# Folding the cast sequence of the first two batches before stage 1 of an FNet + GEGLU kernel, with small tables on ScalarE and idle matmuls between the folds

## The chip, the core and the metric

The kernel runs on one core of one Trainium2 chip. The metric is the device time of one execution in microseconds (us), and lower is better.

The engines are named as in the profile: PE is TensorE (matmuls), PEld its weight loads, DVE is VectorE, ACT is ScalarE, POOL is GpSimd, SP is SyncE.

## The reference

```python
def _attn_ref(x):                       # x: [8, 3008, 256] float32
   X = np.fft.fft(x, axis=1)            # along the sequence
   X = np.fft.fft(X, axis=2)            # along the channels
   return X.real.astype(np.float32)

def _moe_ref(x, w_gate, w_val, w_out):  # x: [24064, 256], d_ff = 1536
   g = x @ w_gate
   gelu = 0.5 * g * (1.0 + erf(g * inv_sqrt2))
   val = x @ w_val
   return (gelu * val @ w_out).astype(np.float32)
```

The second function gets the result of the first as 24,064 tokens of 256 channels.

## The kernel before

For each of the 8 batches the kernel makes the Fourier transform by matmuls, in steps:

1. *Stage 1* is the first part of the sequence transform. It contracts over 94 rows of x (3008 = 94 × 32), with a table `G` of sines and cosines. It ends in a buffer `A_sb`.
2. The *channel stage* (`ch`) combines the halves of the channels with small identity matrices `II`, while it swaps rows and columns. It ends in `Z_sb`.
3. `tp_e`, `tp_o` and `tp_y` finish the transform with a table `TP`. They end in `EO_sb` and `EB_sb`.
4. The feed-forward part runs in 36 slots per batch: gate matmuls (`ps_g`), value matmuls (`ps_v`), and in between the second layer (`ps_o`) of the chunk before. The channel transform is multiplied into the weights by `make_w`, from a table `CW`.

The opening does batch 0's transform alone, because nothing else can run yet. From then on a list of "fill" and "pool" work per slot puts the transform of the next batch between the matmuls of the feed-forward part. The time at which the first gate matmul starts is therefore a good measure of the opening.

Batches 2 to 7 are *folded* on POOL before stage 1: the sequence transform of real data has a symmetry that lets the kernel add and subtract each row x and its mirrored row, and each channel and its mirrored channel, and then contract half as much. Batches 0 and 1 are not folded. Their x is cast to bf16 on the way in (`xb`, forward rows and mirrored rows), and stage 1 does the sum inside PE, with two matmuls per row group, the second one with mirrored rows and with a `G` whose one half is negated:

```python
    G = const_pool.tile([NP, NJ, 2, 4 * NK], BF16)      # [..., 0, :] and a negated copy in [..., 1, :]

    def s1(b, jg, half, hl, engine="A"):
        def run():
            ...
            for q, js in enumerate(JG[jg][2 * half : 2 * half + 2]):
                for j in js:
                    for i in range(2):                  # i = 0: forward rows, 1: mirrored rows
                        src = _sub(xb[b], [[1, 128]], (i * NJ + (16 - j if i else j)) * C + hl * 128, part_num=NP)
                        nc.tensor.matmul(
                            _sub(ps, [[192, 2], [1, 96]], q * 96), src, _sub(G, [[96 * i, 2], [1, 96]], j * 192),
                            start=(j == js[0] and i == 0), stop=(j == js[-1] and i == 1))
            ...                                         # evict 128x384 to A_sb on ACT or DVE
```

The opening of the kernel before, cut:

```python
        pool_consts(); index_consts(0); cast_mirror(0, 9, 8)       # POOL: constants and DMA issues
        index_consts(1); cast_mirror(0, 0, 1); cast_forward(0, 1, 8)
        pool_consts2()                                             # the row "par" for the TP table
        cast_mirror(0, 5, 4); cast_mirror(0, 1, 4)
        ...                                                        # weights
        for _ in range(12):                                        # idle matmuls
            nc.tensor.matmul(ps[:, :], idle[:, 0:128], idle[:, :], start=True, stop=True)
        vec_consts(); g_phases(); vec_fills()                      # DVE
        g_sin(9, 7); g_sin_ends(); g_sin(1, 8)                     # ACT
        stage_cast(9, 4, 0); stage_cast(13, 4, 4); stage_cast(0, 1, 8); g_negative(9, 8)    # DVE
        t_columns(); t_phases(); ...; cw_phases(); ...
        stage1(2, 0); stage1(2, 1); identities(); stage1(3, 0); stage1(3, 1)
        cw_rest(); t_write()
        stage1(1, 0); stage1(1, 1); stage1(0, 1); stage1(0, 0)
        ch(0, 0)(); ch(0, 1, "V")(); make_w(0, 0, 256, engine="V")(); ...
```

"Idle matmuls" multiply a zeroed tile and are thrown away. They serve only to keep PE busy.

## Time and profile before

| | before |
|---|---|
| time, median of the 3 runs given | 646.64 us (646.18 to 647.09) |
| span of the profiled execution | 644.7 us |
| PE busy | 628.5 us, 97% of the span |
| first gate matmul starts | 28.17 us |
| granted clock 0.50 | from 9.9 to 27.0 us, and before 6.5 us |
| stage 1 of batch 0 | 68 matmuls, 9.70 to about 21.5 us |

Part 4 of the page of the kernel before is the chain of waits: the work that ended last, followed back. Its first line gives shares of the span by engine.

```profile
PE 86%; ACT 4%; POOL 3%; DVE 2%; DMA 2%; issue 1%; SPq 0%; ACTq 0%; POOLq 0%; DVEq 0%
```

PE sets the time. The next view has the windows of the kernel before: each line is a stretch of 10 us, with the busy time and the number of instructions of PE, PEld, DVE, ACT and POOL, then the granted PE clock, the DMA share and GB/s.

```profile
10.00:20.00 10.00, 9.21 (x59) 8.36 (x57) 7.98 (x31) 5.03 (x11) 8.96 (x12) 0.50 0.97 131
20.00:30.00 10.00, 8.89 (x65) 6.73 (x64) 4.64 (x7) 4.09 (x10) 0.00 (x0) 0.65 1.14 185
...
60.00:70.00 10.00, 9.70 (x78) 7.13 (x78) 6.51 (x11) 7.93 (x18) 4.40 (x4) 1.00 0.20 39
70.00:80.00 10.00, 10.00 (x82) 6.83 (x80) 8.81 (x14) 7.16 (x15) 7.50 (x8) 1.00 0.98 243
```

From 70 us on, PE is busy. So whatever a change of the first two batches gains, it gains before 70 us. Between 10 and 20 us PE seems 92% busy, but at half its clock: a busy PE is not a fast PE. The timeline of PE in the opening of the kernel before shows it; its columns are start and duration in us, engine, line, operation, out<-in, shape, number of instructions, and, in brackets, the idle time ahead and what ended it.

```profile
1.19 5.30 PE L753 MATMUL ps_o<-gelu_sb 128*128 128x512 bf16 x12 [1.19 <-DVE col L295]
8.50 1.27 PE L364 MATMUL ps_v<-one,par 1*128 1x1 f32 x10 [2.00 <-POOL par L272]
9.70 0.64 PE L463 MATMUL ps_g<-G,xb 94*128 94x192 bf16 x4
...
20.68 0.84 PE L463 MATMUL ps_g<-G,xb 94*128 94x192 bf16 x4
...
22.18 0.93 PE L488 MATMUL ps_v<-II,A_sb 128*128 128x129 bf16 x7 [0.42 <-DVE A_sb L471]
...
28.17 0.61 PE L621 MATMUL ps_g<-EO_sb,W_sb 128*128 128x512 bf16 x2
```

Groups of four stage-1 matmuls start 0.64 us apart, 160 ns for each. Batch 1's stage 1 has the same matmuls, in between the feed-forward work and at the full clock. Two lines of it, from the same view later on:

```profile
49.42 0.49 PE L463 MATMUL ps_dft<-G,xb 94*128 94x192 bf16 x4 [0.58 <-ACT A_sb L469]
50.83 0.83 PE L463 MATMUL ps_dft<-G,xb 94*128 94x192 bf16 x8
```

Four more matmuls take 0.34 us longer, about 85 ns for each by these rounded lines; the starts in the trace are 82 ns apart, and 68 of them are 5.6 us of PE. The first line also shows PE waiting for an eviction of stage 1. All waits of PE between 42 and 75 us in the kernel before (columns: who waits, for what, total us, times, longest):

```profile
PE ps_dft L463 <- ACT A_sb L469: 1.2, 2, 0.6
PE ps_dft L568 <- ACT W_sb L420: 0.7, 1, 0.7
PE ps_dft L463 <- ACT EO_sb L553: 0.5, 1, 0.5
PE ps_dft L463 <- ACT EB_sb L571: 0.3, 1, 0.3
```

### The profile page before, as it was taken

The numbers are of one execution on the slowest core, as the hardware profiler recorded it, in microseconds if no ns is written. First come the engines' busy times: TensorE is split into PE (matmuls) and PEld (weight loads), VectorE is DVE, ScalarE is ACT, GpSimd is POOL, SyncE is SP. The second block draws the span as 40 slices with busy tenths as digits, with TensorE's granted clock in tenths as the row PEclk, the third lists the DMA queues.
The fourth block names the chain that finished last, engine by engine and source line by source line (L and its number), as shares of the span: only waits on it lengthen the run. The fifth ranks groups of instructions, "written<-read, shape, count | busy, mean of one in ns | idle before, by whom it ended". The sixth has DMA issues, their size and how long they took to land.

```text
span 644.7 us, 13198 instructions
## 1 busy us (share of the span) xinstructions
PE 628.5 (97%) x4381; PEld 420.7 (65%) x4381; DVE 586.0 (91%) x944; ACT 434.4 (67%) x852; POOL 496.8 (77%) x498
## 2 busy tenths in 40 slices
PE   7988999999999999999999999999999999999997
PEld 4645767666666666666666666666666666666666
DVE  8587888999989999999999999999999999999992
ACT  4587777676676667776776667766677666666661
POOL 8174699979988799978998799987998655556651
PEclk8699999999999999999999999999999999999999
DMA  8950736444526425533445436463222332221223
GB/s 154 150 81 2 190 104 154 116 110 111 140 62 171 120 49 149 135 103 107 109 97 146 99 99 148 94 152 95 56 53 45 93 93 58 58 46 35 49 50 79
DMA packets 51994, 63.85 MB, mean 99 GB/s; under 512 B 7783, under 2 KB 47194, under 8 KB 49530
## 3 DMA queue, kind: packets, MB, share of 16 engines
q1 hardware_dynamic: 45238, 47.23, 30.3%
q0 software_dynamic: 6096, 15.29, 11.5%
q8 instruction: 34, 0.56, 0.4%
q10 hardware_dynamic: 592, 0.49, 0.3%
q14 instruction: 34, 0.28, 0.1%
HBM read 38.86 MB, written 29.38 MB: 106 GB/s over the span
## 4 chain that ended last, share of the span: by engine, by line
PE 86%; ACT 4%; POOL 3%; DVE 2%; DMA 2%; issue 1%; SPq 0%; ACTq 0%; POOLq 0%; DVEq 0%
PE ps_o L694 35%; PE ps_g L621 27%; PE ps_v L621 17%; PE ps_dft L507 2%; DMA out_dram<-out_sb 2%; PE ps_dft L543 1%; ACT gelu_sb L637 1%; POOL eo_sb L214 1%; POOL h_sb L670 1%; PE ps_dft L463 1%; ACT gelu_sb L646 1%; PE ps_dft L488 1%; DVE v_sb L668 1%; PE ps_dft L410 1%; PE ps_dft L573 0%
## 5 line engine op out<-in xcount | busy, mean ns | idle before, releaser
L670 POOL TENSOR_TENSOR h_sb<-gelu_sb,v_sb 128x512 bf16<-128x512 bf16 (+1 forms) x288 | 329.7, 1147 | 129.1 <-DVE v_sb L668 96.4
L694 PE MATMUL ps_o<-Wo_sb,h_sb 128*128 128x256 bf16 (+1 forms) x2232 | 334.7, 273 | 0.0
L694 PEld LDWEIGHTS <-h_sb 128*128 128x128 bf16 (+1 forms) x2304 | 228.8, 100 | 111.0 <-POOL h_sb L670 1.5
L655 DVE SCALAR_TENSOR_TENSOR ve_sb<-EB_sb,yw,ps_v 128x512 f32<-128x512 bf16 (+1 forms) x288 | 212.4, 737 | 37.8 <-PE ps_v L621 36.2
L637 ACT ACTIVATE gelu_sb<-ps_g 128x512 bf16<-128x512 f32 (+1 forms) x288 | 169.6, 589 | 92.7 <-PE ps_g L621 92.0
L621 PE MATMUL ps_g<-EO_sb,W_sb 128*128 128x512 bf16 (+1 forms) x864 | 230.7, 376 | 0.8 <-ACT gelu_sb L646 0.5
L621 PE MATMUL ps_v<-EO_sb,W_sb 128*128 128x512 bf16 (+1 forms) x576 | 214.5, 375 | 0.0
L666 DVE TENSOR_TENSOR h_sb<-gelu_sb,ps_v 128x512 bf16<-128x512 bf16 (+1 forms) x288 | 195.4, 678 | 0.6 <-PE ps_o L694 0.3
L668 DVE SCALAR_TENSOR_TENSOR v_sb<-ve_sb,ps_v 128x512 f32<-128x512 f32 (+1 forms) x288 | 192.9, 670 | 0.0
L621 PEld LDWEIGHTS <-W_sb 128*128 128x128 bf16 x1440 | 137.0, 98 | 77.9 <-issue 1.6
L646 ACT ACTIVATE gelu_sb<-ps_g 128x512 bf16<-128x512 f32 (+1 forms) x288 | 168.4, 585 | 0.0
L713 ACT ACTIVATE out_sb<-ps_o 128x512 f32<-128x512 f32 x92 | 55.0, 597 | 34.5 <-PE ps_o L694 33.9
L214 POOL TENSOR_TENSOR eo_sb<-ab_sb 94x512 bf16<-94x512 f32 (+1 forms) x60 | 66.6, 1111 | 0.1
L510 ACT ACTIVATE S_sb<-ps_dft 96x512 bf16<-96x512 f32 x48 | 28.2, 588 | 21.0 <-PE ps_dft L507 21.0
L553 ACT ACTIVATE EO_sb<-ps_dft 128x512 bf16<-128x512 f32 (+1 forms) x44 | 26.0, 591 | 23.2 <-PE ps_dft L543 21.2
L207 POOL TENSOR_TENSOR ab_sb<-x_raw,x_raw 94x508 f32<-94x508 f32 (+1 forms) x30 | 33.0, 1101 | 0.0
L210 POOL TENSOR_TENSOR ab_sb<-x_raw,x_raw 94x508 f32<-94x508 f32 (+1 forms) x30 | 33.0, 1099 | 0.0
L507 PE MATMUL ps_dft<-eo_sb,G 94*96 94x256 bf16 x102 | 19.2, 274 | 1.8 <-POOL eo_sb L214 1.2
L158 POOL DMA_INDIRECT x_raw<-in_x_dram,idx x18 | 17.1, 949 | 2.9 <-issue 1.1
L463 PEld LDWEIGHTS <-xb 94*128 94x128 bf16 x136 | 15.4, 121 | 4.7 <-issue 3.6
L543 PE MATMUL ps_dft<-TP,Z_sb 128*128 128x128 bf16 (+1 forms) x184 | 17.6, 218 | 0.4 <-ACT W_sb L416 0.4
L543 PEld LDWEIGHTS <-Z_sb 128*128 128x128 bf16 x192 | 15.1, 100 | 2.1 <-issue 0.3
(127 smaller groups left out, 188.9 us busy)
## 6 DMA issues: line engine op xcount, KB each, us to landing
out_dram<-out_sb SPq DMA_DIRECT2D x361, 64.0 KB
x_raw<-in_x_dram SPq DMA_DIRECT2D x10, 768.0 KB
Z_sb<-z SPq DMA_DIRECT2D x6, 768.0 KB
z<-S_sb SPq DMA_DIRECT2D x6, 576.0 KB
EB_sb<-yrow SPq DMA_DIRECT2D x14, 128.0 KB
x_raw<-in_x_dram SPq DMA_DIRECT2D x2, 640.0 KB
z<-S_sb SPq DMA_DIRECT2D x6, 192.0 KB
EB_sb<-yrow SPq DMA_DIRECT2D x7, 120.2 KB
```

Source lines behind the costliest of these rows:

```text
L207: eng.tensor_tensor(ab(0, 1, up), fwd(1, up), mir(255, down), op=ALU.add)
L214: eng.tensor_tensor(_sub(eo, [[C, nj], [1, 128]], j0 * C + g * 128), ab(0, 0, [[1, 128]]), ab(1, 0, [[1, 128]]), op=op)
L543: nc.tensor.matmul(ps[:, o : o + n], st["Z"][:, pair, g * 128 : g * 128 + 128], _sub(TP, [[1, n]], g * 128), start=True, stop=True)
L621: nc.tensor.matmul(ps[:, :n], W[nm, part][:, fs], src, start=start, stop=stop, **kw)
L637: nc.scalar.activation(gl[:, 0, :n], pg[:, :n], AF.Gelu)
L646: nc.scalar.activation(_sub(gl, [[-1, n]], TOK + n - 1), pg[:, :n], AF.Gelu)
L655: nc.vector.scalar_tensor_tensor(ve[:, :n], EB_bufs[b][:, c0 : c0 + n], yw[:, fc : fc + 1], pv[:, :n], op0=ALU.mult, op1=ALU.add)
L666: nc.vector.tensor_tensor(st["h"][:, fc, 0, :n], gl[:, 0, :n], pv[:, :n], op=ALU.mult)
L668: nc.vector.scalar_tensor_tensor(_sub(vv, [[-1, n]], n - 1), ve[:, :n], 2.0, pv[:, :n], op0=ALU.mult, op1=ALU.subtract)
L670: nc.gpsimd.tensor_tensor(st["h"][:, fc, 1, :n], gl[:, 1, :n], vv[:, :n], op=ALU.mult)
L694: nc.tensor.matmul(pso[:m, half], st["h"][:, fc, sign, h0 : h0 + m], Wo_sb[:, fc, :], start=(fc == 0), stop=(fc == NFC - 1),)
L713: nc.scalar.activation(_sub(osb, [[1, 2 * C]], 0, part_num=m), pso[:m, :], AF.Copy)
```

## The change

The intent is to fold batches 0 and 1 too, so that their stage 1 has half as many matmuls with half as many columns. DVE folds batch 0 in the opening, POOL folds batch 1 in slots 6 to 18. To make room on DVE, the small tables (identities, parts of `CW`, `TP`) move to ACT, and 24 more idle matmuls keep PE busy while DVE folds (36 in all). `par` is made earlier on POOL. The channel stage of these two batches takes the folded halves with half as many matmuls of twice the columns, and batch 2's loads and first folds move by two or three slots. The core of the diff:

```diff
-    G = const_pool.tile([NP, NJ, 2, 4 * NK], BF16)
+    G = const_pool.tile([NP, NJ, 4 * NK], BF16)
@@ fold_ops: batches 0 and 1 write a and b straight to eo
+        half = b < 2
+            if half:
+                return _sub(eo, [[C, nj]] + pat, j0 * C + q * 128 + c0)
+        if half:
+            return [first, second]
         return [first, second, combine(0, ALU.add), combine(1, ALU.subtract)]
@@ s1
-                    for i in range(2):
-                        src = _sub(xb[b], [[1, 128]], (i * NJ + (16 - j if i else j)) * C + hl * 128, part_num=NP)
-                        nc.tensor.matmul(
-                            _sub(ps, [[192, 2], [1, 96]], q * 96), src, _sub(G, [[96 * i, 2], [1, 96]], j * 192),
-                            start=(j == js[0] and i == 0), stop=(j == js[-1] and i == 1))
+                    nc.tensor.matmul(
+                        ps[:, q * 96 : (q + 1) * 96], eo[:, j, g, :], G[:, j, :],
+                        start=(j == js[0]), stop=(j == js[-1]))
@@ identities: on ACT
-            nc.vector.tensor_scalar(II[:, i, 0:128], row, col_p, sign, op0=ALU.is_equal, op1=ALU.mult)
+        nc.scalar.activation(eye, row_c, AF.Abs, scale=-1.0, bias=col_p)
+        nc.scalar.activation(II[:, 0, 0, :], eye, AF.Relu, scale=-1.0, bias=1.0)
... (CW and TP likewise)
@@ opening
         cast_mirror(0, 9, 8)
+        pool_consts2()
         index_consts(1)
         cast_mirror(0, 0, 1)
         cast_forward(0, 1, 8)
-        pool_consts2()
...
-        for _ in range(12):
-            nc.tensor.matmul(ps[:, :], idle[:, 0:128], idle[:, :], start=True, stop=True)
+        warm(9)
+        vec_fills()
         vec_consts()
         g_phases()
...
+        t_sin()
+        warm(15)
         cw_phases()
         cw_sin()
...
+        t_write()
         identities()
         cw_rest()
+        fold_piece(9, 4)
+        stage1(2)
+        warm(4)
+        fold_piece(13, 4)
+        fold_piece(0, 1)
+        stage1(3)
+        warm(5)
+        fold_piece(5, 4)
+        stage1(1)
+        warm(3)
+        fold_piece(3, 2)
+        fold_piece(1, 2)
+        stage1(0)
@@ plan
+        slot_of = [6 + i * 13 // len(ops) for i in range(len(ops))]     # batch 1's folds on POOL
-        for k, s in ((0, 16), (1, 16), (2, 17)):
+        for k, s in ((0, 18), (1, 19), (2, 19)):
             at(fill, s, lambda k=k: load_part(2, k))
-            first, n = (s0 - 16, 29) if b == 2 else (s0 - 22, 32)
+            first, n = (s0 - 13, 29) if b == 2 else (s0 - 22, 32)
```

## The prediction

> **What bounds the kernel now.** From about 70 us on, TensorE (PE) has no gaps (windows view: 10.00 busy in every 10 us; the chain of waits is 86% PE), and the change leaves that part's matmuls alone. What can move is the first 70 us (timeline):
> - x arrives by DMA (mean DMA share about 1.0 from 5 to 30 us). Stage 1 of batch 0 is 68 matmuls, 94x192, from 9.7 to 21.5 us, 160 ns start to start: half speed. The granted clock is 0.50 from 9.9 to 27.0 us.
> - 22.2 to 28.2 us: channel stage, W tables, transposes; the first gate matmul (ps_g) starts at 28.17 us.
> - Batch 1's stage 1, between 48 and 69 us at full clock: 68 matmuls at about 82 ns = 5.6 us of PE, and PE waits about 2 us for evictions (A_sb, EO_sb, EB_sb) around them.
>
> **What the change does.**
> - Stage 1 of batches 0 and 1: 34 matmuls of 96 columns each. The 128-column matmuls of the channel stage, a weight load each, run at about 56 ns, so I estimate 34 x 56 = 1.9 us, against 5.6.
> - Batch 1: 8 evictions of 128x384 instead of 16 on ACT, and about 12 us of folds on POOL (1.26 us per 94x508 operation, as L207), in slots where POOL is 45 to 65% busy.
> - Batch 0: DVE loses the casts of stage (2.8 us), negatives (0.74), identities and CW (1.7), TP (0.54), seven evictions (3.9); it gains the folds. The 94x408 fp32 operation took 0.57 us, so I estimate 0.65 per 508 elements, 1.3 per four-row piece, 6 us in all.
> - par comes earlier on POOL, so the remaining DMA issues come about 2 us earlier.
> - 24 more idle matmuls on PE. The Trainium skill (TensorE: Matmul & The Clock Gate, Part 1) says activity over a window of about 3.4 us lifts the clock from half to full, and idleness drops it. The trace agrees in the levels (12 idle matmuls at 427 ns each, later 512-column ones at 217) and the window (0.50 lasts 17.07 us, five times 3.41), but 94-row matmuls streaming from 14 to 21 us did not lift it. I expect mostly full clock from about 10 us.
>
> **The critical path after.** DVE reaches the folds at about 9 us and ends them at 15 to 15.5, near the arrival of the last mirrored rows (13 to 14). Last A_sb eviction: 16.3. Channel stage to first gate takes about 4.5 us at full clock instead of 6.0: first gate at 20.5 to 22 us, 6 to 7.5 earlier. W rows from 512 land about 22 to 23 us (bytes over GB/s), just in time. Batch 1 gains 3.5 to 5 us more. The dense rest keeps its length; I allow 1 us for new POOL waits.
>
> **Predicted: 636.0 us (-1.6%), range 631.0 to 641.0. Faster by over 2%: 0.28; within 2%: 0.71; slower: 0.01.**
>
> **What would show each step.** First ps_g at 20.5 to 22 us; granted clock 1.0 between 10 and 27 us; DVE folds at 9 to 15.5 us, about 0.6 us per large operation; stage 1 of batch 1 near 2 us of PE; DVE, not PE, before the last stage-1 matmuls; gapless PE from 70 us.
>
> **What would make it wrong.** The clock stays at 0.50 (then the idle matmuls delay stage 1: +2 to 3 us); weights land late and the gain turns into waits for w_raw; POOL folds lag, holding h_sb or batch 1's stage 1; DVE folds slower beside POOL; batch 2's later loads and folds stall PE near 100 us.

## The result and the profile after

| | before | after |
|---|---|---|
| time, median (range), 4 runs each | 646.41 us (646.10 to 647.09) | 635.34 us (634.99 to 635.73) |
| ratio | | 0.9828 (95% interval 0.981 to 0.9845) |
| span of the profiled execution | 644.7 us | 633.9 us |
| first gate matmul | 28.17 us | 22.70 us |

The change makes the kernel 1.7% faster. That is less than the 2% at which a verdict of "faster" begins, so its class is "same"; but the whole interval lies below 1, so the gain is clear of the noise. The outputs are right.

The two timelines can be laid side by side at the start of each gate matmul group, which both kernels have in the same order (289 starts). The table gives the start in the kernel before, and how much earlier the kernel after is at the same group. It is worked out from the two timelines.

| gate group | before | after | earlier by |
|---|---|---|---|
| 0 | 28.17 | 22.70 | 5.47 |
| 8 | 46.81 | 41.28 | 5.53 |
| 12 | 57.30 | 48.69 | 8.61 |
| 20 | 78.02 | 66.74 | 11.28 |
| 28 | 95.56 | 85.60 | 9.96 |
| 72 | 189.80 | 178.83 | 10.97 |
| 288 (end) | 628.88 | 618.01 | 10.87 |

The gain has two parts of almost the same size: 5.5 us in the opening, and about 5.4 us while batch 1's transform runs. After that the difference wavers between 9.7 and 11.5 us and ends at 10.87.

**The opening.** The timeline of PE in the kernel after, to compare with the one of before:

```profile
1.19 4.02 PE L757 MATMUL ps_o<-gelu_sb 128*128 128x512 bf16 x9 [1.19 <-DVE one L290]
5.27 2.29 PE L371 MATMUL ps_v<-one,par 1*128 1x1 f32 x10
7.49 6.02 PE L757 MATMUL ps_o<-gelu_sb 128*128 128x512 bf16 x15
13.34 0.34 PE L467 MATMUL ps_g<-G,eo_sb 94*128 94x96 bf16 x4
...
16.40 0.81 PE L757 MATMUL ps_o<-gelu_sb 128*128 128x512 bf16 x3
17.05 0.34 PE L467 MATMUL ps_g<-G,eo_sb 94*128 94x96 bf16 x4
17.22 0.33 PE L467 MATMUL ps_v<-G,eo_sb 94*128 94x96 bf16 x4
18.19 0.61 PE L489 MATMUL ps_dft<-II,A_sb 128*128 128x256 bf16 x4 [0.64 <-ACT A_sb L473]
...
22.70 0.61 PE L622 MATMUL ps_g<-EO_sb,W_sb 128*128 128x512 bf16 x2
```

Stage 1 now starts 3.6 us later (13.34 against 9.70), but ends 4 us earlier. From the channel stage to the first gate it takes 4.51 us instead of 6.0, because the clock is full. A note on reading the clock: the page shows a clock of 1.00 from the start of this execution, but that is only because the record begins with its first change. The idle matmuls of line 1 ran 427 ns apart, which is half speed. The first recorded change is at about 12.8 us, and the 15 idle matmuls of line 3 agree: at 427 ns each they would take 6.4 us, at 213 ns 3.2 us, and they took 5.85 us until stage 1.

Ahead of stage 1 stand DVE's folds. DVE's timeline in the kernel after, cut:

```profile
3.67 1.36 DVE L322 TENSOR_SCALAR ff<-ff 94x24 f32<-94x24 f32 x1
...
7.59 0.16 DVE L372 COPY parc<-ps_v 128x5 f32<-128x5 f32 x1 [0.90 <-PE ps_v L371]
...
11.02 0.68 DVE L217 TENSOR_TENSOR eo_sb<-x_stage,xb 94x508 bf16<-94x508 f32 x1
11.62 0.68 DVE L220 TENSOR_TENSOR eo_sb<-xb,x_stage 94x508 bf16<-94x508 bf16 x1
...
14.50 0.41 DVE L217 TENSOR_TENSOR eo_sb<-xb 94x508 bf16<-94x508 bf16 x1
14.84 0.41 DVE L220 TENSOR_TENSOR eo_sb<-xb 94x508 bf16<-94x508 bf16 x1
...
16.06 0.28 DVE L220 TENSOR_TENSOR eo_sb<-xb 94x254 bf16<-94x254 bf16 x1
```

The folds begin at 10.93 us and end at 16.34. A large fold operation costs 0.60 us start to start where one input is fp32, and 0.34 us where both are bf16. Two delays ahead of them stand out. The wait for `parc` is one: PE's ten small matmuls that make it ran at half clock and took 2.29 us, against 1.27 before. The first line is the other: 94x24 elements took 1.36 us. The same operation in the kernel before, and the instruction of POOL that runs beside it after:

```profile
2.60 0.17 DVE L311 TENSOR_SCALAR ff<-ff 94x24 f32<-94x24 f32 x1
```

```profile
3.44 1.56 POOL L281 IOTA par<- 1x128 f32 x1
```

POOL's instruction runs from 3.44 to 5.00 us, and DVE's ends at 5.03. The Trainium skill ("SBUF — State Buffer", section "Who interferes with whom") says that DVE and GpSimd share a pair of ports, that `tensor_scalar` can take it in its two-port modes, and that "whoever issues first gets the shared pair for the whole instruction". The trace agrees: 1.36 us beside that IOTA, 0.17 us without it. Moving `par` forward on POOL put it beside this operation. The kernel before has such a clash elsewhere: beside its own `par` IOTA, DVE's cast of 96x1024 elements took 1.83 us, and the next one of the same size 0.79 us.

The two delays don't add up. `parc` could not be ready before PE's `par` matmuls ended, at 7.56 us. The slow 94x24 operation lies ahead of the wait for it: without the 1.19 us that it lost, DVE would have waited 2.1 us instead of 0.9, and the folds would have begun at the same time.

At the other end, ACT's timeline of the kernel after shows the first and the last eviction of stage 1 there:

```profile
15.38 0.47 ACT L473 ACTIVATE A_sb<-ps_g 128x384 bf16<-128x384 f32 x1
...
17.61 0.53 ACT L473 ACTIVATE A_sb<-ps_g 128x384 bf16<-128x384 f32 x1
```

The first result of stage 1 was there at about 13.7 us, but ACT made tables until 15.38 and then evicted seven times without a pause. The last two evictions, on ACT and on DVE, ended at 18.15. So it is ACT's queue that sets the start of the channel stage, and not the folds. The chain of waits of the kernel after, from the view that follows it back from the last instruction (start, us, engine, tile, line, number), goes through ACT, and no fold is on it:

```profile
5.27 2.30 PE ps_v L371 x10
...
10.32 0.44 DVE small L261
10.78 0.42 ACT CW L349
...
15.48 2.66 ACT A_sb L473 x7
18.19 0.61 PE ps_dft L489 x4
```

ACT starts its tables when DVE's `small` table is there, DVE makes that after `parc`, and `parc` comes from the `par` matmuls. PE ran without a gap from 7.49 to 17.55 us, so it never waited for a fold: each group of stage 1 came 0.7 to 1.6 us after its fold was ready, behind idle matmuls. Three of these (0.65 us) stand between the last fold (16.34) and the last stage-1 group (17.05). The run e1 below takes the later idle matmuls away, and ACT's evictions and the channel stage stay where they are.

**Batch 1.** One line of PE's timeline in the kernel after, and PE's waits there between 42 and 75 us:

```profile
53.80 0.34 PE L467 MATMUL ps_dft<-G,eo_sb 94*128 94x96 bf16 x4
```

```profile
PE ps_g L622 <- ACT gelu_sb L647: 1.2, 3, 0.6
PE ps_dft L467 <- ACT EB_sb L572: 0.7, 1, 0.7
```

Stage-1 matmuls are now 43.5 ns apart (groups of five take 0.38 us, of four 0.34), so 34 of them are 1.5 us instead of 5.6. That is 4.1 us. PE's waits in these 33 us fall from 2.7 to 1.9 us. Together that is 4.9 of the 5.4 us; I don't place the last half microsecond.

**What comes back.** Two windows of the kernel after:

```profile
70.00:80.00 10.00, 10.00 (x74) 6.66 (x73) 8.51 (x13) 7.73 (x16) 6.43 (x8) 1.00 1.01 261
80.00:90.00 10.00, 9.67 (x74) 6.63 (x73) 8.50 (x14) 6.74 (x15) 10.00 (x10) 1.00 0.29 81
```

PE has no gap from 60 us on but one of 0.33 us near 83 us (and one of 1.2 us near 124 us, which the kernel before has as well, near 128). That gap comes from POOL, whose waits between 70 and 130 us have this line:

```profile
POOL ab_sb L216 <- DMA x_raw<-in_x_dram,idx: 2.0, 1, 2.0
```

In the kernel before the same wait is 0.5 us. POOL is ready for batch 2's fold before the gather of its mirrored rows has landed, and then runs late with `h_sb`.

### The profile page after: what moved, and what is told of

Same layout as the page of the kernel before. It is cut to its first block, busy times and chain, and to the rows that moved or that the text cites. A ratio compares the mean times of both kernels' runs of the same rounds, so it can differ in the third digit from the quotient of the medians. Undisturbed runs are those within 1.5% of the kernel's fastest.

```text
span 633.9 us, 13022 instructions
## 1 busy us (share of the span) xinstructions
PE 620.3 (98%) x4289; PEld 409.6 (65%) x4289; DVE 582.4 (92%) x937; ACT 433.0 (68%) x855; POOL 505.8 (80%) x511
## 3 DMA queue, kind: packets, MB, share of 16 engines
q0 software_dynamic: 6096, 15.29, 11.5%
## 4 chain that ended last, share of the span: by engine, by line
PE 85%; POOL 5%; ACT 5%; DVE 3%; issue 1%; POOLq 0%; ACTq 0%; DVEq 0%
PE ps_o L695 35%; PE ps_g L622 27%; PE ps_v L622 17%; POOL h_sb L671 3%; PE ps_dft L508 2%; PE ps_dft L544 2%; DVE v_sb L669 1%; ACT gelu_sb L638 1%; POOL eo_sb L224 1%; ACT gelu_sb L647 1%; PE ps_dft L489 1%; PE ps_dft L574 0%; DVE ve_sb L656 0%; ACT W_sb L423 0%; ACT A_sb L473 0%
## 5 line engine op out<-in xcount | busy, mean ns | idle before, releaser
L757 PE MATMUL ps_o<-gelu_sb 128*128 128x512 bf16 x36 | 13.1, 529 | 1.2 <-DVE one L290 1.2
```

## The experiments

Theories are told in words here; the quoted expectations give some of them letters. "First gate" is the start of the first gate matmul in the profiled execution, and "end" is the start of the last gate group against the kernel before. All kernels but one gave right results.

### e1_no_idle: the changed kernel without the later idle matmuls

The theory (A in the quotes) is that the idle matmuls earn their place by lifting the clock for the channel stage. The rival is that they only stand in front of stage 1.

```diff
-        warm(15)
         cw_phases()
         ...
         stage1(2)
-        warm(4)
         fold_piece(13, 4)
         fold_piece(0, 1)
         stage1(3)
-        warm(5)
         fold_piece(5, 4)
         stage1(1)
-        warm(3)
```

> The changed kernel without its 27 later idle matmuls (only the first nine stay). Theory A (the idle matmuls carry the clock): the granted clock stays 0.50 until about 25 us, the part from channel stage to first gate takes about 6 us again instead of 4.5, first ps_g at 24 to 25 us instead of 22.7, time 1 to 2.5 us longer than the changed kernel, about 637. Rival B (they only hold the queue: stage 1 began at 13.34 us although its first fold was ready at 12.3): first ps_g up to 1 us earlier, time about 634.5.

Measured: 637.91 us (636.86 to 638.12), ratio 0.985 (0.9833 to 0.9867), so about 0.2% worse than the changed kernel's 0.9828 (1.4 us by the ratios, 2.6 us by the medians of different rounds). The two intervals overlap, so the traces have to carry the reading. Two lines of PE's timeline in e1_no_idle:

```profile
11.77 0.50 PE L467 MATMUL ps_g<-G,eo_sb 94*128 94x96 bf16 x4 [4.20 <-DVE eo_sb L217]
...
18.20 1.03 PE L489 MATMUL ps_dft<-II,A_sb 128*128 128x256 bf16 x4 [1.30 <-ACT A_sb L473]
```

Stage 1 began 1.6 us earlier, at 11.77, as the rival says. But the channel stage began at the same time (18.20 against 18.19), and the way from there to the first gate took 6.0 us instead of 4.5, at half clock: first gate 24.19 against 22.70. So the idle matmuls delay stage 1, that delay costs nothing, and the clock that they bring is worth 1.5 us at the first gate. The delay costs nothing because ACT is later still: its seven evictions began at 15.40 us in e1 and the last at 17.62, against 15.38 and 17.61, and PE stood 1.30 us for them. At the end e1 is 8.49 us ahead of the kernel before, 2.4 us less than the change; part of the rest is PE's wait behind batch 2's gather, 1.2 us instead of 0.33. One of the four executions (636.86 us, mean clock 0.988 against 0.998 or 0.999) had another course of the clock; see e8_early_rows below.

### e2_before_idle: the kernel before with 15 more idle matmuls

This asks what the clock alone is worth, without any fold.

```diff
         gelu_table()
+        ps = psum("o")
+        for _ in range(15):
+            nc.tensor.matmul(ps[:, :], idle[:, 0:128], idle[:, :], start=True, stop=True)
         stage1(2, 0)
```

> The kernel before with 15 idle matmuls ahead of its unfolded stage 1 and nothing else. Theory A (half of the gain of the opening is the clock, not the folding): clock 1.0 from about 13 us, stage 1 at 82 ns a matmul, 5.6 us instead of 10.9, first ps_g near 24 us instead of 28.2, time about 642.5. Rival B (the opening's gain comes from halving stage 1): stage 1 only starts later, first ps_g at 28 us or later, time 646 to 649.

Measured: 645.11 us, ratio 0.9969 (0.9951 to 0.9988). One line of PE's timeline in e2_before_idle:

```profile
14.63 0.49 PE L463 MATMUL ps_g<-G,xb 94*128 94x192 bf16 x4
```

The clock was full from about 13.4 us. Stage 1 ran at 83 ns per matmul instead of 160, but began at 14.63 instead of 9.70, and ended at about 20.8 us. First gate 25.90, 2.27 us earlier; end 1.56 us earlier. I had expected more from the clock alone. A faster stage 1 is worth 5.2 us (68 × 77 ns), and 4.9 of it are paid for by its later start, behind the queue of idle matmuls. What remains is mostly the way from the channel stage to the first gate, 4.2 us (from 21.70) instead of 6.0. In the changed kernel the channel stage has to wait for ACT anyway (e1), so the idle matmuls cost nothing there.

### e3_fold1_only and e4_fold0_only: each batch's fold alone

e3 has the old opening and batch 0 unfolded, and batch 1 folded on POOL; e4 has the new opening, and batch 1 as before (its tables are made on POOL when that is idle).

```diff
 e3:
-        half = b < 2
+        half = b == 1
 e4:
-        half = b < 2
+        half = b < 1
 (both: old stage 1 and channel stage kept beside the new ones, as s1_old and ch_old; old G, old identities as I3)
```

> Batch 1 alone folded (on POOL), the opening of batch 0 as before. If the two parts add up: first ps_g at 28.2 us as before, and the 5.3 us that the changed kernel gains after its first gate stay, time about 641.2. Rival: those 5.3 us come in part from the earlier opening (data and weights there sooner), then under 3 us of gain, time 643.5 or more.

> Batch 0 alone folded with the idle matmuls, batch 1 unfolded as before (its tables made on POOL while that is idle). If the parts add up: first ps_g at 22.7 us, gain about 5.5 us kept to the end, time about 641. Rival: the opening's gain is swallowed by later waits when batch 1's stage 1 is unfolded, gain under 3.5 us, time 643 or more.

| | time | ratio | first gate earlier by | end earlier by |
|---|---|---|---|---|
| e3 (batch 1) | 641.28 us | 0.9912 (0.9893 to 0.9931) | -0.25 us | 5.21 us |
| e4 (batch 0) | 640.54 us | 0.9892 (0.9875 to 0.9908) | 5.19 us | 5.26 us |
| both (the change) | 635.34 us | 0.9828 (0.981 to 0.9845) | 5.47 us | 10.87 us |

The parts add up: 5.21 and 5.26 are 10.47 us, against 10.87. The ratios agree within their noise: gains of 0.88% and 1.08% are 1.96%, against 1.72%, with intervals of about 0.2% each. In e4 the difference stays between 5.19 and 5.41 us at every gate group, so nothing of the opening's gain is lost later. In e3 it is -0.25 us until group 8 and then grows to 5.53 by group 20. The 5.4 us of the result are batch 1's fold, as read.

### e5_idle94 and e6_idle192: what an idle matmul needs to lift the clock

In the kernel before, 68 dense matmuls of stage 1 (94 rows) did not lift the clock from 9.9 to 21.5 us. The rows theory (R in the quotes) says that matmuls over 94 of the 128 rows don't count enough. The columns theory (C) says that it is their 192 columns, too short for PE to be busy throughout. e5 keeps the 512 columns and takes 94 rows; e6 keeps the 128 rows and takes 192 columns, in 8/3 as many matmuls.

```diff
 e5:
-                nc.tensor.matmul(ps[:, :], idle[:, 0:128], idle[:, :], start=True, stop=True)
+                nc.tensor.matmul(ps[:, :], idle[:NP, 0:128], idle[:NP, :], start=True, stop=True)
 e6:
-            for _ in range(n):
-                nc.tensor.matmul(ps[:, :], idle[:, 0:128], idle[:, :], start=True, stop=True)
+            for _ in range(n * 8 // 3):
+                nc.tensor.matmul(ps[:, 0:192], idle[:, 0:128], idle[:, 0:192], start=True, stop=True)
```

> The changed kernel, its idle matmuls over 94 rows instead of 128 (same count, same 512 columns). Theory R (a matmul over 94 rows, like stage 1 of batches 0 and 1, does not lift the clock): clock stays 0.50 until after 20 us, the 15 idle matmuls run at 427 ns to 13.9 us, stage 1 and the channel stage at half speed, first ps_g at 24.5 us or later, time as without them or worse, 637.5 to 639. Rival C (it is the short 192-column matmuls with their gaps that do not): as the changed kernel, clock full from about 12 to 13 us, time within 0.5 us of it.

> The changed kernel, its idle matmuls over 128 rows but 192 columns each (8/3 as many, so the same columns). Theory R: clock full from about 12 to 13 us as in the changed kernel, time within 0.5 us of it. Rival C: clock stays 0.50 until after 20 us, time 637.5 to 639.

e5: 640.94 us, ratio 0.9906 (0.9889 to 0.9922); first gate 28.09. e6: 636.11 us, ratio 0.9836 (0.9819 to 0.9853); first gate 21.73. Two lines of PE's timeline in e5_idle94:

```profile
7.49 6.58 PE L757 MATMUL ps_o<-gelu_sb 94*128 94x512 bf16 x15
13.86 0.53 PE L467 MATMUL ps_g<-G,eo_sb 94*128 94x96 bf16 x4
```

In e5 PE had no gap from 7.5 to 21.9 us, and yet the clock rose only at about 27 us, after the 128-row matmuls of the channel stage, which began at 22.2. In e6 it rose at about 4 us. So 94 rows against 128 make the difference, and 192 columns against 512 don't: theory R holds, C falls. With idle matmuls that don't lift the clock the opening's gain is gone (0.08 us left): they stand in front of stage 1 at half speed, so that it ended at about 21.9 us instead of 17.55, and the rest of the opening stays slow as well.

e6's first gate came 1 us earlier than in the changed kernel, but its time is no better. It was 12.26 us ahead of the kernel before at group 20, and 9.28 at group 28. The gather of batch 2 landed after 12.8 us (11.5 in the changed kernel), POOL stood 3.7 us for it and PE 2.0 us for POOL. What is won in the opening is partly given back there.

### v1_opening: another order of the opening

An attempt to beat the change: the first fold and its stage 1 before the `TP` and `CW` tables, the identities first on ACT, `par` made after the forward rows' DMA is issued, row 0 last, 12 idle matmuls at first.

```diff
+        fold_piece(9, 4)
         t_columns()
         ...
-        warm(15)
+        warm(3)
+        stage1(2)
         cw_phases()
         ...
+        warm(14)
         fold_piece(13, 4)
-        fold_piece(0, 1)
-        stage1(3)
         fold_piece(5, 4)
         stage1(1)
         ...
+        fold_piece(0, 1)
+        stage1(3)
```

> The changed kernel with its opening reordered: the forward rows and the mirrored ones are asked for before the column constants where nothing needs those first, the first fold comes before the table phases on DVE, the identities at the head of ScalarE, 12 idle matmuls first (so that the clock can rise near 6.5 us), column groups in the order of arrival. Theory (DVE and the arrival of the mirrored rows at 14.4 us set the end of the folds): folds end at 14.5 instead of 16.3 us, first ps_g at 20 to 21 us instead of 22.7, time 633 to 634. Rival (the weights' arrival sets the pace once the first gate comes before 22 us): first ps_g earlier, but the third gate pair no earlier than 25.5 us, time 635.

Measured: 636.25 us, ratio 0.9835 (0.9819 to 0.9852), first gate 22.59: no gain. One line of DVE's timeline in v1_opening says why:

```profile
8.13 0.19 DVE L216 TENSOR_TENSOR eo_sb<-x_stage,xb 94x8 bf16<-94x8 f32 x1 [2.64 <-DMA xb<-in_x_dram,idx]
```

DVE was ready early and stood for 2.64 us, until the first mirrored rows had landed at 8.1 us; the tables that could have filled this time came after, and the last piece was folded at 17.2. My miss was to move a fold ahead of data that were not there.

### v2_later_fold2: a failed schedule

This is v1_opening with the first fold of batch 2 one slot later, against the wait for its gather.

```diff
-            first, n = (s0 - 13, 29) if b == 2 else (s0 - 22, 32)
+            first, n = (s0 - 12, 29) if b == 2 else (s0 - 22, 32)
```

> The reordered opening, and batch 2's first fold one slot later, so that POOL does not stand 2.0 us at 76 us waiting for rows of x, with h_sb products behind it. If that wait costs what PE shows (0.33 us before ps_o at 83 us): 0.3 us better than the reordered opening alone. Rival: PE is fed anyway, or the later folds lengthen the 1.2 us stall on eo_sb at 124 us: 0 to 1 us worse.

The result was wrong (relative error 0.147), so its time (644.38 us, ratio 0.9955) tells nothing. Worked out from the slots, and not tested by a run: batch 2's last use of `eo` in stage 1 slips to slot s0+17, in which batch 3's fold writes `eo` and is emitted first. The program is then free of races, but in the wrong order. Only the comparison of the result found it.

### e7_tables_dve: the small tables back on DVE

The theory (D) says that the move of the tables to ScalarE is worth about 2 us, because DVE is on the path to the folds. The Trainium skill ("ScalarE: Activation LUTs", section "Rules for kernel authors") advises the other way for such simple operations: for `relu`, `add` and `mul`, VectorE and not ScalarE. The trace agrees that VectorE is faster: DVE made these tables in 1.8 us in e7 (9.94 to 11.71), ACT in 2.8 us in the changed kernel (12.61 to 15.38).

```diff
-        nc.scalar.activation(eye, row_c, AF.Abs, scale=-1.0, bias=col_p)
-        nc.scalar.activation(II[:, 0, 0, :], eye, AF.Relu, scale=-1.0, bias=1.0)
+        nc.vector.tensor_scalar(II[:, 0, 0, :], row_c, col_p, None, op0=ALU.is_equal)
 (CW and TP likewise)
```

> The changed kernel with its small tables (identities, CW columns, TP) written by DVE as before, ahead of the folds, not by ScalarE. Theory D (the folds on DVE set the time of stage 1, so DVE is the engine to relieve): about 2 us of table work goes in front of the folds, they end at 17.5 to 18.3 us instead of 16.3, first ps_g 1 to 1.8 us later, time 636.2 to 637.2. Rival S (ScalarE, busy with tables until 15.4 us and then with eight evictions until 18.1, sets it): first ps_g no later, time within 0.4 us of the changed kernel or better.

Measured: 637.31 us (635.69 to 638.09), ratio 0.9847 (0.9832 to 0.9861). The interval overlaps that of the change (0.981 to 0.9845): a cost of 1 to 2 us, not a sure one. In the profiled execution the folds began at 11.71 us and ended at 16.55 (theory D had expected 17.5 to 18.3), and the first gate came at 23.47, 0.77 us later than in the changed kernel. Two lines of PE's timeline in e7_tables_dve show that this difference is not the tables' alone:

```profile
6.62 3.41 PE L756 MATMUL ps_o<-gelu_sb 128*128 128x512 bf16 x15
12.54 0.50 PE L466 MATMUL ps_g<-G,eo_sb 94*128 94x96 bf16 x4 [2.50 <-DVE eo_sb L217]
```

Here the clock rose at about 5.6 us, not at 12.8. The 15 idle matmuls were over at 10.0, PE stood for 2.5 us, and the clock fell back from 12.4 to 15.9 us. This is the next point.

### e8_early_rows: batch 2's forward rows loaded early

This is the changed kernel, with the loads of batch 2's forward rows moved from slots 18 and 19 to slots 10 and 12. The theory (G) says that the gather of mirrored rows lands late because the forward rows share the DMA with it.

```diff
+        for k, s in ((0, 10), (1, 12), (2, 12)):
+            at(fill, s, lambda k=k: load_forward(2, *PARTS[k]))
         for k, s in ((0, 18), (1, 19), (2, 19)):
-            at(fill, s, lambda k=k: load_part(2, k))
+            at(fill, s, lambda k=k: load_mirror(2, *PARTS[k]))
```

> The changed kernel with only the forward rows of batch 2 asked for at slots 10 and 12 instead of 18 and 19 (their buffer is free since the opening), the gathers of the mirrored rows unchanged. Theory G (the gather for batch 2 takes 11.2 us from issue to landing beside those loads, POOL stands 2.0 us for it at 76 us and h_sb reaches PE late): the gather lands in 8 to 9 us, POOL's wait at that place falls under 0.5 us, PE's 0.33 us wait before ps_o at 83 us goes, time 0.3 to 0.5 us shorter, about 635.0. Rival: the gather is slow by itself, landing stays at 11 us, no gain.

Measured: 642.69 us, ratio 0.9934 (0.9921 to 0.9948): 7 us worse than the change. The mechanism was right: the gather landed in 6.2 us instead of 11.5, POOL did not wait for it, and PE not for POOL. But one line of PE's timeline in e8_early_rows shows a new wait that is far larger:

```profile
31.33 1.03 PE L419 MATMUL ps_dft<-w_raw,CW 128*128 128x512 bf16 x2 [6.61 <-DMA w_raw<-in_moe_w_val_dram]
```

What SyncE's queue waited for before these loads were the opening's DMAs and, last, DVE's last fold of batch 0, which frees their buffer. It ended at 15.85 us, so they went out at 15.88, beside the weights, not in slot 10 (in v3 below, 14.90 and 14.93). A place in the program is not a place in time, unless something gates it.

The opening of this kernel is instruction by instruction that of the changed kernel, and so is a second reading of it. The first lines of PE's timeline in e8_early_rows:

```profile
5.27 1.27 PE L373 MATMUL ps_v<-one,par 1*128 1x1 f32 x10 [0.48 <-POOL par L286]
6.47 3.41 PE L759 MATMUL ps_o<-gelu_sb 128*128 128x512 bf16 x15
```

Four kernels begin with the same 9 idle matmuls, the same ten for `par` and the same 15 idle ones on PE:

| | clock rises at about | `par` matmuls | folds begin | first gate |
|---|---|---|---|---|
| e8_early_rows | 4.2 us | 1.27 us | 9.95 us | 21.72 us |
| e7_tables_dve | 5.6 us | 1.42 us | 11.71 us (tables on DVE) | 23.47 us |
| the change | 12.8 us | 2.29 us | 10.93 us | 22.70 us |
| e4_fold0_only | 13.5 us | 2.29 us | 10.99 us | 22.98 us |

The Trainium skill ("TensorE: Matmul & The Clock Gate", Part 1) says that the window of 3.4 us over which the activity is judged is free-running and doesn't start with the kernel. The records agree: 3.41 us is the distance of two changes of the clock in the kernel before and in e2 and e7, or a multiple of it, and the same instructions get a full clock 9 us earlier or later. Counting windows back from these four rises, the ones that lifted early had about 3.0 us (e8) and 2.8 us (e7) of the first idle matmuls inside one window, and the best window of the change and of e4 had 2.5 and 2.1 us. These last numbers are an estimate, worked out from the starts above and the 427 ns of each matmul. So 9 idle matmuls, 3.8 us at half clock, lift the clock in some executions and not in others. An early rise makes the `par` matmuls 1 us faster, DVE gets `parc` without a wait, and the folds begin 1 us earlier (e8). It moves the first gate by about 1 us, and by way of ACT: in e8 and e6 ACT's last eviction began at 16.62 and 16.63 instead of 17.61, the first gate came 0.98 and 0.97 us earlier, but the last fold ended only 0.49 and 0.21 us earlier, since DVE waited for rows (0.89 and 1.15 us). What an early rise does to the whole time is not shown: the four timed executions of the change lie within 0.74 us, and nothing says in which of them the clock rose early. I made no run that varies only the number of the first idle matmuls.

This also changes what e6 and e7 say. e6's 1 us at the first gate is what an early rise gives to e8 as well, with the changed kernel's own idle matmuls. And e7 against e8, both with an early rise, is 1.75 us at the first gate, near the 2 us of theory D; against the change it is 0.77. But the clock is mixed into both numbers: in e7 it was back at half from 12.4 to 15.9 us, and the four idle matmuls ahead of stage 1's second group took 1.70 us, against 0.86 in the changed kernel. So what the tables cost on DVE at an equal clock is open, in time as well, as the intervals overlap. Theory D and rival S each hold in one kernel. With the tables on ACT, ACT's queue sets the channel stage; with the tables on DVE, ACT had gaps between its evictions and waited for PE (1.34, 1.62 and 0.71 us), and the folds and PE behind them set it. Whether following the page's advice would pay here is not shown.

### v3_opening_rows and v4_opening_rows_s1: a better opening, with the early rows

v3 has another opening: all the tables that need no late data go ahead of the first fold, row 0 is last, and the early rows of e8 are in it. v4 adds one slot to one group of batch 2's stage 1, against the wait of 1.2 us near 124 us.

```diff
 v3:
         g_phases()
+        cw_phases()
+        identities()
         g_sin(9, 7)
         ...
+        warm(7)
         fold_piece(9, 4)
         stage1(2)
+        warm(8)
         fold_piece(13, 4)
         fold_piece(5, 4)
         stage1(1)
         ...
+        fold_piece(0, 1)
+        stage1(3)
 v4:
-                ready = slot_of[piece * per + per - 1] + 1
+                ready = slot_of[piece * per + per - 1] + 1 + (b == 2 and i == 2)
```

> Opening reordered a second time (on DVE the table phases come in the time before the first mirrored rows land at about 8.1 us, then all folds in a row; the constants row no longer beside DVE copies), with the early rows of the run before. Theory: folds end at 13.5 to 14 us instead of 16.3, first ps_g at 19 to 20 us instead of 22.7, and as the gather no longer holds batch 2 this stays to the end: time 632 to 633.5. Rival (weights): first ps_g as early, but the third pair of gates waits for W rows from 512 that land near 22 to 23 us, time 634 to 635.

> As the run before, with the third column group of batch 2's stage 1 one slot later, where PE stands 1.2 us on eo_sb (at 124 us in the changed kernel, 128 us in the one before). Theory: that wait goes, 1.0 to 1.2 us shorter than the run before. Rival: the wait moves to the next user of eo_sb or Z_sb, no gain.

v3: 641.33 us, ratio 0.9906 (0.989 to 0.9921). v4: 640.43 us, ratio 0.9902 (0.9886 to 0.9917). The new order did what it was made for: most folds ended at 13.4 us, the last piece at 14.9, and the first gate came at 20.29, which is 2.4 us earlier than in the changed kernel. ACT's tables came earlier as well: its first eviction was at 12.33 instead of 15.38. (DVE's 94x24 operation took 0.17 us here, with `par` elsewhere on POOL.) Then the early rows cost a wait of 7.8 us for `w_raw` in v3 and 7.1 us in v4, as in e8. v4's extra slot took away the wait of 1.2 us: between groups 44 and 48 v4 loses 0.45 us against the kernel before, and v3 1.81. Whether v3's opening without the early rows, or with rows that something holds back, beats the change was not run. e6 warns that some of it would be given back at batch 2's gather.

No run beat the changed kernel.

## Why the prediction was right, point by point

The predicted time was 636.0 us, the measured one 635.34. That the sum came so near is in part luck: two terms were off in opposite directions.

- **What bounds the kernel: right.** PE has no gap after 60 us but 0.33 and 1.2 us, and the gain is all made before.
- **"Batch 1 gains 3.5 to 5 us more": a bit small.** It gave 5.4 us (5.2 to 5.5 in e3 alone). The term that was mis-sized is "34 x 56 = 1.9 us": the 96-column matmuls came 43.5 ns apart, 1.5 us in all. The waits for evictions fell as expected, by 0.8 us.
- **"First gate at 20.5 to 22 us, 6 to 7.5 earlier": too much.** It came at 22.70, 5.47 us earlier. Two steps failed. "DVE reaches the folds at about 9 us": it was 10.93, because `parc` was there only at 7.56 us, after ten matmuls at half clock; the 94x24 operation, 1.19 us longer beside POOL's IOTA, was hidden ahead of that wait. And the path: the prediction had the folds set the last eviction, and wanted to see "DVE, not PE, before the last stage-1 matmuls". PE never waited for DVE there, and ACT's queue set the last eviction (next but one point). The folds themselves cost what was predicted, 0.60 us for a large one, and even 0.34 where both inputs are bf16.
- **"Mostly full clock from about 10 us": late.** It was about 12.8 us in this execution. The same opening got it at 4.2 us in e8. The prediction cited the page on the clock for the window, but left out that the window is free-running.
- **"Last A_sb eviction: 16.3": it was 18.15.** ACT made its tables until 15.38, because they begin with DVE's `small` table at 10.78, and then needed 2.8 us for seven evictions. The prediction had not looked at ACT's queue. The folds ended 0.8 to 1.3 us late, too, and three idle matmuls stood between the last fold and the last stage-1 group (0.65 us), but e1 shows that this did not count: without them ACT's last eviction began at 17.62.
- **"About 4.5 us at full clock instead of 6.0": right.** It was 4.51, and e1 gives 6.0 at half clock.
- **"The remaining DMA issues come about 2 us earlier": wrong, and without effect.** The last two gathers were issued at 8.93 and 10.21 us, against 9.01 and 10.29. There was no wait for the weights in the changed kernel.
- **"I allow 1 us for new POOL waits": about right in kind.** POOL waits 2.0 us for batch 2's gather instead of 0.5, and 0.33 us of it reach PE. e6 shows how this grows when the opening gets faster.

What is shown by experiments: the two parts and their independence (e3, e4), the worth of the clock (e1, e5), that 94 rows don't lift it where 128 do (e5, e6), and that an earlier stage 1 alone doesn't bring the channel stage forward (e1). What is only read from traces: ACT as the engine that holds it (the chain of waits, with e6 and e8 in agreement), the clash on the shared ports, the phase of the clock's window. Open: the worth of the tables on ScalarE, what ACT's tables made earlier would bring by themselves, and half a microsecond of batch 1's gain.

## What to carry to other kernels

Idle matmuls that are to lift the clock should fill the array's rows (94 of 128 were not enough here) and last well over one window, and they pay where PE waits for another engine anyway; put ahead of ready work they cost about what they bring. When work moves to a new engine or a new place, look up what runs beside it at that time: an operation of 0.17 us took 1.36 us, and loads that were moved early in the program ran as soon as their buffer was free and held up the weights, for which PE then stood 7 us. Look also at what that engine has to do next: ACT, with the tables, came late to its evictions, and that set the opening. A faster opening only counts as far as the next thing that the DMA must bring in time.

## What the Trainium skill lacked or had wrong

- "TensorE: Matmul & The Clock Gate" doesn't say that the rows of a matmul count. Dense matmuls over 94 rows did not lift the clock in 14 us (e5), while matmuls over 128 rows with 192 columns lifted it at about 4 us (e6).
- The same page says that a profile holds the clock's transitions, but doesn't warn that the time before the first one is then unknown; the views used here count it as full. The changed kernel's page shows full clock from the start, while its first idle matmuls ran 427 ns apart and the first change is at about 12.8 us. That its window is free-running, which the page says, is seen here: 4.2, 5.6, 12.8 and 13.5 us for the same first instructions.
- "VectorE: DVE Perf Modes", Mode 2×_1P, asks for 4-byte alignment. The bf16 fold operations start at an odd bf16 element, and one operand runs backward; they still came 0.34 us apart for 94x508 elements, against 0.60 us with one fp32 input. Another page of the skill, "Vector Engine (DVE) Microarchitecture Reference", has it right in section 5.1: alignment makes no difference.
- No page gives the cost of an IOTA on GpSimd. The one with a four-level pattern took 1.48 to 1.56 us for 1x128 elements, the one with a simple pattern 0.23 us for 128x128 (0.55 us in one place, where a cast of DVE ran beside it).
- No page gives how long an indirect gather takes to land beside other loads. The same three gathers of batch 2 had a median of 6.2 us (e8), 11.5 us (the change) and 12.8 us (e6).
